# Attention stage: the keys' largest projection goes into their exponentials as a bias, four copies become reciprocals, the rest rows use another PSUM bank, and the first two steps are in an order written by hand

## The chip, the core and the metric

The kernel runs on one core of one Trainium2 chip. The metric is the device time of one execution, in microseconds (us); the median of a few executions is given. A core has five engines with a queue each, which work in their queue's order: TensorE (PE, matrix products and transposes), VectorE (DVE), ScalarE (ACT), GpSimd (POOL) and SyncE (SP, which issues the transfers here). They wait for each other by semaphores. PE writes its results to PSUM, which has eight banks of 128 x 512 float32.

## The reference

```
def phi(x):
    proj = x @ w_phi                                   # 64 -> 128 features
    proj = proj - max(abs(proj), axis=-1)              # per row
    return concat([exp(proj), exp(-proj)], -1)         # 256 features
q_p, k_p = phi(q), phi(k)                              # 4 batches, 8 heads, 576 rows
kv  = k_p^T v ;  z = sum of k_p over the rows
attn = (q_p kv) / (q_p z + 1e-6)                       # -> x, 2304 x 512
x = max(x w1, x w2, x w3) @ w_out                      # first expert layer, d_ff 768
... noisy top-2 routing of x to 8 experts, each relu(x w1[e]) w2[e], weighted sum ...
```

The weights of the layer behind the attention arrive as 64-bit numbers. The kernel makes 32-bit ones of them while the attention runs ("narrowing").

## The kernel before

The program has three stages: linear attention, the first expert layer, and the routed experts. The change touches the first alone, some 220 us of the whole.

**Steps.** The attention runs in 16 steps, one for each batch and pair of heads; `period(a)` lists what step `a` issues. Each call is entered with a time (`at(t, f, ...)`); the calls are sorted by these times, and that sorted list is the order of the queues of PE, DVE, ACT and SP. The times set an order only; nothing waits for a clock. In one period three steps overlap: step `a` is projected, step `b = a - 1` is summed into kv and z, and step `c = a - 2` gets its numerators, denominators and the division. Of the 576 rows of a head, 512 go through each step ("main rows"); the last 64 rows of two batches are put together and handled once in two steps ("rest rows", kind "r"): their projection and exponentials of the keys in the even steps, the transposition of their queries (`turn_q` of kind "r") in the odd ones.

**The path of a step.** `turn` transposes the loaded rows (PE, into a PSUM bank), `raw_in` copies them to the tile `th` (ACT), `proj` multiplies by `w_phi` (PE, keys into the banks p0 and p1, queries into s0 and s1, rest rows into s2 and t1). `peak` takes the largest absolute value of each row (DVE, tile `m`), `center` subtracts it (DVE, tiles `dk`, `dq`, `dr`). For keys, `exp_k` takes the exponentials of `dk` and of `-dk` (ACT, tile `kp`, four instructions of 128 x 512 in a step). For queries, `turn_q` transposes `dq` (PE) and `exp_q` takes the exponentials (ACT). `kv_sum` and `z_sum` sum over the rows (PE, bank k), `kv_out`, `kv_turn` and `kv_in` copy and transpose the sums (`kvT`, `kv`).

**The division.** `denom` puts the denominators into bank t0, `den_in` copies them (ACT, tile `dn`), and a chain on DVE follows: `den_turn` (a transpose, `dt`), `den_inv` (a reciprocal, `rc`), `den_copy` (four small copies within `rc`), and then twice `den_back` (`rb`) and `divide` (into `xT`), once for the numerators in bank s2 and once for those in t1. A bank that holds numerators is free when its `divide` has read it.

**Narrowing.** For each half block of the weights, SP loads `bits`, DVE makes `nm` in two instructions, ACT makes `nr`, and POOL needs four more (`narrow_end`); `narrow_out` then stores the result, or, for the first eight halves, splits it into `wh` (ACT) and `wl` (POOL). An odd step from step 3 on has two halves, an even one has one.

The banks that matter here, and the lines of the calls that the change moves:

```
A_, B_, C_, D_, E_, G_, H_ = "p0", "p1", "s0", "s1", "t0", "s2", "t1"
at(1.65, turn, a, "r", G_)            # even step: rest rows, into s2
at(2.2, turn_q, b, "r", 0, G_)        # odd step: their queries, into s2
at(8.9, numer, c, 0, G_)              # numerators, into s2
```

Of the kernel before, what the change touches and what calls it, by code (L numbers as in the profile page):

```python
# [9 lines left out]
F32 = mybir.dt.float32  # L10
# [4 lines left out]
AF = mybir.ActivationFunctionType  # L15
# [4 lines left out]
P = 128  # L20
# [3 lines left out]
class Plan:  # L24
# [5 lines left out]
    def at(self, t, f, *x):  # L30
        self.ops.append((t, len(self.ops), f, x))
# [7 lines left out]
def tile_linear_attention__then__moe__then__noisy_top2_moe(  # L39
# [20 lines left out]
    nc = tc.nc  # L60
# [17 lines left out]
    HALF = S // 2  # L78
# [11 lines left out]
    plan = Plan()  # L90
    at = plan.at
    st, pools = {}, {}
# [216 lines left out]
    ap, ain = pools["attn"], pools["ain"]  # L309
# [61 lines left out]
                         v[b, 2 * hp + h, 0:MAIN, :].rearrange("(p j) d -> p j d", j=JT))  # L371

    kps, qps = {}, {}

    def heads(s):
        u, i = divmod(s, 2)
        bb, hp = divmod(u, HP)
        return u, i, bb, hp
# [38 lines left out]
    def width(kind):  # L417
        return 2 if kind == "r" else 4
# [7 lines left out]

    def center(s, kind, g):
        n = width(kind)
        pj, m = st.pop(("pj", kind, g))[:, :n], st.pop(("m", kind, g))
        if kind == "r":  # L430
            if g == 0:
                st["d", kind] = ap.tile([P, 4, NF], F32, name="dr").rearrange(
                    "p (a h) f -> p a h f", a=2)
            d = st["d", kind][:, :, g, :]
        else:
            d = ap.tile([P, 4, NF], F32, name=f"d{kind}", bufs=2)
            st["d", kind, g] = d
        nc.vector.tensor_tensor(d, pj, m[:, :, None].to_broadcast([P, n, NF]), op=ALU.subtract)  # L438

    def exp_k(s, kind, g, sg):  # L440
        u, i, bb, hp = heads(s)
        scale = 1.0 - 2.0 * sg
        if kind == "r":
            if sg == 0:
                kps[u, "r"] = ap.tile([P, 2, 2, NF], F32, name="kp2", bufs=2)
            nc.scalar.activation(kps[u, "r"][:, :, sg, :], st["d", kind][:, 0], AF.Exp, scale=scale)
            return
        if g == 0 and sg == 0:
            kps[s] = ap.tile([P, 2, 4, 2, NF], F32, name="kp4", bufs=2)
        nc.scalar.activation(kps[s][:, g, :, sg, :], st["d", kind, g], AF.Exp, scale=scale)  # L450

    def turn_q(s, kind, g, name):
        pt = bank(name).rearrange("p (a c) -> p a c", a=4)
# [71 lines left out]
    def quarter(h, n):  # L525
        g = 2 * h + n
        return slice(g * QD, (g + 1) * QD)
# [24 lines left out]

    def den_inv(s):
        rc = ap.tile([P, 2, NB], F32, name="rc", bufs=2)
        dt_ = st.pop(("dt", s))[:, 0:HALF:32]
        nc.vector.reciprocal(rc, dt_[:, None, :].to_broadcast([P, 2, NB]))
        st["rc", s] = rc

    def den_copy(s, n):

        rc = st["rc", s]
        for h in range(2):
            nc.vector.tensor_copy(rc[quarter(h, 1 - n), n, :], rc[quarter(h, n), n, :])

    def den_back(s, n):
        rb = ap.tile([P, NB, 32], F32, name="rb", bufs=2)
# [9 lines left out]
    NS = B * HP  # L576
    STEP = 10.9
# [35 lines left out]
    def step_halves(a):  # L613

        def count(a):
            return min(a, 1) + (a % 2 if a > 2 else 0)

        n = sum(count(i) for i in range(a))
        return range(n, n + count(a) if a < NS else len(halves))

    A_, B_, C_, D_, E_, G_, H_ = "p0", "p1", "s0", "s1", "t0", "s2", "t1"

    def both(t, kind, a, at):
        for g in range(2):
            at(t + 1.4 * g, peak, a, kind, g)
            at(t + 0.7 + 1.4 * g, center, a, kind, g)

    def den_steps(t, c, at, last=False):
        at(t, den_turn, c)
        at(t + 0.5, den_inv, c)  # L630
        for n in range(2):
            at(t + 0.8, den_copy, c, n)
            at(t + 1.5 + 0.9 * n, den_back, c, n)
            at(t + 2.0 + 0.9 * n, divide, c, n)

    def loads(a, at):
        if 0 < a < NS:
            at(0.0, fill, a)
            if a == 3:
                at(0.0, routing_loads)  # L640
            if a == 2:
                at(2.0, routing_consts)
            if a + 1 < NS:
                at(0.0, load_main, a + 1)
                at(0.0, load_vals, a + 1)
            if a + 1 == 2 * HP:
                at(0.0, load_rest, 1)
        if a == 2 * HP:
            at(7.5, load_rest_v, 1)
        if a < NS:  # L650
            for i, n in enumerate(step_halves(a)):
                at(1.5 + 0.9 * i, narrow_mid, n)
                at(2.8 + 0.9 * i, narrow_end, n)
                at(9.5 + 4.0 * i, narrow_out, n)
            for n in step_halves(a + 1):
                at(8.0, narrow_load, n)

    def period(a):
        base = a * STEP
        b, c = a - 1, a - 2  # L660

        def at(t, f, *x):
            plan.at(base + t, f, *x)

        loads(a, at)
        even = a % 2 == 0
        if not even:
            at(0.0, prepare, b)
        at(0.0, turn, a, "k", A_)
        at(0.1, raw_in, a, "k")  # L670
        at(0.44, turn, a, "q", B_)
        at(0.5, raw_in, a, "q")
        if c >= 0:
            at(0.88, kv_turn, c, D_)
            at(1.0, kv_in, c)
        at(1.2, turn_q, b, "q", 0, C_)
        at(1.3, exp_q, b, "q", 0)
        if even:
            at(1.65, turn, a, "r", G_)
            at(1.7, raw_in, a, "r")  # L680
        at(1.9, turn_q, b, "q", 1, E_)
        at(2.0, exp_q, b, "q", 1)
        if not even:
            at(2.2, turn_q, b, "r", 0, G_)
            at(3.0, exp_q, b, "r", 0)
        at(2.35, proj, a, "k", (A_, B_))
        at(3.25, proj, a, "q", (C_, D_))
        both(3.4, "k", a, at)
        for g in range(2):
            for sg in range(2):  # L690
                at(4.9 + 1.4 * g, exp_k, a, "k", g, sg)
        if even:
            at(4.15, proj, a, "r", (G_, H_))
            for g in range(2):
                at(6.1 + 0.01 * g, peak, a, "r", g)
                at(6.12 + 0.01 * g, center, a, "r", g)
            for sg in range(2):
                at(7.5, exp_k, a, "r", 0, sg)
        both(7.4, "q", a, at)
        at(4.6, kv_sum, b)  # L700
        at(6.8, z_sum, b)
        at(8.0, kv_out, b)
        if c >= 0:
            at(7.9, denom, c, E_)
            at(8.95, den_in, c)
            at(8.9, numer, c, 0, G_)
            at(9.9, numer, c, 1, H_)
            den_steps(10.1, c, at)

    def opening():  # L710

        at(1.2, busy, 12)
        loads(0, at)
        at(4.0, turn, 0, "k", A_)
        at(4.1, raw_in, 0, "k", True)
        at(4.2, busy, 3)
        at(4.3, turn, 0, "q", C_)
        at(4.4, raw_in, 0, "q")
        at(4.5, turn, 0, "r", G_)
        at(4.6, raw_in, 0, "r")  # L720
        at(5.0, proj, 0, "k", (A_, B_))
        at(5.3, proj, 0, "q", (C_, D_))
        at(5.5, proj, 0, "r", (G_, H_))
        both(6.0, "k", 0, at)
        for g in range(2):
            for sg in range(2):
                at(7.0 + 1.4 * g, exp_k, 0, "k", g, sg)
        for g in range(2):
            at(9.0 + 0.01 * g, peak, 0, "r", g)
            at(9.02 + 0.01 * g, center, 0, "r", g)  # L730
        for sg in range(2):
            at(9.3, exp_k, 0, "r", 0, sg)
        both(9.3, "q", 0, at)

    at(0.0, start)
    opening()
    for s in range(1, NS):
        period(s)
    T = NS * STEP

# [709 lines left out]
    for i in range(2 * 4):  # L1450
        g, j = 1 + i // 4, i % 4
        t = END + 0.1 + i * 3.2
# [63 lines left out]
    for c in range(NCHUNK):  # L1516
        if c == 1:
            for i, job in enumerate(jobs):
                t = clock[0] + 8.0 * i
# [55 lines left out]
    for n, (e, M, row0) in enumerate(units):  # L1575
# [9 lines left out]
        if seven(n):  # L1585
            for two in ((0, 1), (2, 3)):
                for q_ in ORDER7:
                    for f in two:
                        pe(2 * 3 * HN / 2400, product, n, e, q_, f)
                        d0, d = (-0.03, 0.01) if two[0] and q_ == ORDER7[-1] else (0.02, 0.44)  # L1590
# [165 lines left out]
```

## Time and profile before

| | |
|---|---|
| median of 3 executions | 991.24 us (990.67 to 992.7) |
| the profiled execution, its own time | 993.33 us |
| its span, first to last instruction | 991.7 us |
| mean granted TensorE clock | 0.985 |
| PE busy | 956.3 us (96%) |
| DVE, ACT, POOL busy | 603.9, 453.4, 487.8 us |

The profile gives each engine's busy time; a busy share is a mean over stages with different limits. Behind the attention PE is busy nearly all the time. In the attention stage no engine is. In rows of the timeline the columns are: start in us, duration of the group in us, engine, line, operation, output<-input, shape, count; in brackets the engine's idle time just before, and what ended it. Several instructions of one form that follow each other stand in one row, with their count.

### The profile page before, as it was taken

Reading aid. Unit: us, or ns where it says so; the run is one execution under the profiler, and the core shown is the slowest. Engines: PE = TensorE matmul, PEld = TensorE weight load, DVE = VectorE, ACT = ScalarE, POOL = GpSimd, SP = SyncE. Lnnn points to the kernel's source line nnn. Section 1 sums busy time; section 2 is a strip of 40 time slices with the busy share of each in tenths; the row PEclk is TensorE's granted clock in tenths of the full one; section 3 lists DMA queues with packets and bytes.
Section 4 is the critical chain, followed back from the end, with each engine's and each line's share of the span. In section 5 each row is a group of like instructions: output and inputs, shape, how many; then the busy total and the mean of one; then the engine's idle time right before and its main releaser. Section 6 shows DMA issues by size and latency. Waiting matters only on the chain. (4 is left out here: it accounts for less than half of the span.)

```text
span 991.7 us, 19004 instructions
## 1 busy us (share of the span) xinstructions
PE 956.3 (96%) x7225; PEld 832.2 (84%) x7225; DVE 603.9 (61%) x1253; ACT 453.4 (46%) x894; POOL 487.8 (49%) x554
## 2 busy tenths in 40 slices
PE   7988889899999999999999999999999999999997
PEld 5766666678999999999998789989898989889895
DVE  4889989996435363636345425547577675756641
ACT  5766566663333333433334314427364554636350
POOL 4656666652126464464423444137374555647253
PEclk9989999999999999999999999999999999999999
DMA  7457476524245756566605355737565564838312
GB/s 202 99 167 191 128 251 187 159 69 150 64 143 174 236 171 223 182 187 189 207 4 182 93 182 165 278 97 280 169 253 193 199 248 157 293 128 302 122 32 70
DMA packets 125359, 169.19 MB, mean 171 GB/s; under 512 B 35630, under 2 KB 86958, under 8 KB 125266
## 3 DMA queue, kind: packets, MB, share of 16 engines
q1 hardware_dynamic: 114338, 138.35, 44.5%
q0 software_dynamic: 10928, 29.62, 8.7%
q8 instruction: 57, 0.93, 0.4%
q14 instruction: 36, 0.29, 0.1%
HBM read 119.38 MB, written 49.14 MB: 170 GB/s over the span
## 5 line engine op out<-in xcount | busy, mean ns | idle before, releaser
L772 PE MATMUL s<-xh,wh 128*128 128x384 f32 x432 | 147.8, 342 | 0.0
L772 PE MATMUL s<-xh,wl 128*128 128x384 f32 x432 | 145.3, 336 | 0.0
L772 PE MATMUL s<-xl,wh 128*128 128x384 f32 x432 | 145.1, 336 | 0.0
L1233 POOL DMA_INDIRECT out_dram<-o,emeta x40 | 47.4, 1185 | 128.4 <-DVE o L1231 64.4
L782 DVE TENSOR_TENSOR a<-s,a 128x384 f32<-128x384 f32 x72 | 39.9, 554 | 90.3 <-PE s L772 88.1
L1306 DVE TENSOR_TENSOR wl<-raw,wh 128x1024 fp32r<-128x1024 f32 x58 | 70.8, 1220 | 30.6 <-ACT wh L1298 26.6
L1223 PE MATMUL p<-wh,hh 128*128 128x512 f32 (+1 forms) x216 | 86.3, 400 | 0.0
L772 PEld LDWEIGHTS s<-xh,wh 128*128 128x128 f32 x432 | 81.2, 188 | 5.6 <-issue 2.2
L1223 PE MATMUL p<-wl,hh 128*128 128x512 f32 (+1 forms) x216 | 85.2, 395 | 0.0
L1223 PE MATMUL p<-wh,hl 128*128 128x512 f32 (+1 forms) x216 | 85.2, 394 | 0.0
L772 PEld LDWEIGHTS s<-xl,wh 128*128 128x128 f32 x432 | 81.2, 188 | 1.5
L772 PEld LDWEIGHTS s<-xh,wl 128*128 128x128 f32 x432 | 81.1, 188 | 0.0
L1298 ACT ACTIVATE wh<-raw 128x1024 fp32r<-128x1024 f32 x58 | 61.2, 1057 | 34.3 <-DMA raw<-in_moe_w_dram 20.0
L1276 POOL TENSOR_TENSOR raw<-raw 128x256 f32<-128x256 f32 x24 | 19.2, 800 | 110.6 <-DMA raw<-in_moe_w_dram 94.7
L210 POOL TENSOR_TENSOR nm<-nm,nr 128x512 int32<-128x512 int32 x24 | 31.4, 1309 | 73.5 <-ACT nr L202 43.7
L948 POOL DMA_INDIRECT meta<-mt,si x36 | 36.8, 1021 | 54.1 <-DVE si L944 45.0
L1081 PE MATMUL s<-gx,wh 128*128 128x304 f32 x288 | 62.1, 302 | 0.0
L130 ACT ACTIVATE hh<-a 128x384 fp32r<-128x384 f32 x36 | 18.8, 523 | 89.1 <-DVE a L782 89.1
L131 DVE TENSOR_TENSOR gx<-t,gx 128x512 fp32r<-128x512 f32 (+3 forms) x82 | 39.4, 495 | 32.8 <-ACT gx L130 32.7
L130 ACT ACTIVATE gx<-t 128x512 fp32r<-128x512 f32 (+3 forms) x82 | 34.9, 449 | 44.5 <-DVE t L1056 28.3
L1010 POOL DMA_INDIRECT gx<-x2d,emeta x28 | 28.3, 1011 | 47.9 <-PE t L1020 17.5
L450 ACT ACTIVATE kp<-dk 128x512 f32<-128x512 f32 x64 | 36.9, 629 | 30.3 <-DVE dk L438 30.3
(299 smaller groups left out, 2628.3 us busy)
## 6 DMA issues: line engine op xcount, KB each, us to landing
raw<-in_moe_w_dram SPq DMA_DIRECT2D x58, 512.0 KB
raw<-in_moe_w_dram SPq DMA_DIRECT2D x48, 256.0 KB
sums<-qh SPq DMA_DIRECT2D x24, 512.0 KB
sums<-raw SPq DMA_DIRECT2D x24, 512.0 KB
wh<-sums SPq DMA_DIRECT2D x24, 512.0 KB
wl<-sums SPq DMA_DIRECT2D x24, 512.0 KB
bits<-in_moe_w_dram SPq DMA_DIRECT2D x18, 512.0 KB
out_dram<-zrow SPq DMA_DIRECT2D x9, 512.0 KB
```

Of the source, the lines that this page charges most:

```text
L130: nc.scalar.activation(hi, src, AF.Copy)
L131: nc.vector.tensor_tensor(lo, src, hi.bitcast(F32), op=ALU.subtract)
L210: nc.gpsimd.tensor_tensor(m_, m_, r_, op=ALU.add)
L450: nc.scalar.activation(kps[s][:, g, :, sg, :], st["d", kind, g], AF.Exp, scale=scale)
L772: nc.tensor.matmul(p_, a[:, d, fs], b_, start=(n == 0), stop=(n == 3 * KD - 1))
L782: nc.vector.tensor_tensor(a, p_, st.pop("a"), op=ALU.max)
L948: ins = nc.gpsimd.indirect_dma_start(out=meta, out_offset=bass.IndirectOffsetOnAxis(ap=si[:, t, kk:kk + 1], axis=0), in_=mt[:, t, kk, :], ...
L1081: nc.tensor.matmul(bk["p"], a[:, d, fs], b_[:, d, :], start=(d == 0 and i == 0), stop=(d == 1 and i == 2))
L1223: nc.tensor.matmul(p_, a, b_[:, fw], start=(f == 0 and r == 0), stop=(f == (3 if seven(n) else F2 - 1) and r == 2))
L1233: alone(e, nc.gpsimd.indirect_dma_start(out=out, out_offset=bass.IndirectOffsetOnAxis(ap=mt[:m, i, 1:2], axis=0), in_=o[:m], in_offset=Non ...
L1298: nc.scalar.activation(WE[e, i][0], st["w2", e, i], AF.Copy)
L1306: nc.vector.tensor_tensor(wl, st.pop(("w2", e, i)), wh.bitcast(F32), op=ALU.subtract)
```

## The change

Line numbers of the kernel after are 1 to 13 higher in this part than before (`exp_k`'s new exponentials are L462, the new copy of `m` is L433).

- **Keys from step 2 on (`FOLD = 2`).** `center` no longer subtracts on DVE. ACT makes `w = -m` (128 x 4), and `exp_k` reads the projection from its PSUM bank and takes `exp(x + w)` and `exp(-x + m)`, with `w` or `m` as the bias of the ACTIVATE. A bias holds one value for each partition, so an instruction covers 128 columns instead of 512: sixteen instead of four in a step. The banks p0 and p1 stay taken until these are done, and so does the tile `m` (four buffers).
- **Reciprocals for copies.** `den_copy` took four copies of 32 x 9 from `rc`; now it takes four reciprocals of 32 x 9 from `dt`.
- **Rest rows in bank k.** `turn` and `turn_q` of kind "r" write to bank k, not to s2; in odd steps `turn_q` and `exp_q` of the rest rows stand earlier in the step.
- **Steps 0 and 1.** Step 1 is taken out of `period` and interleaved by hand with step 0.
- **Split of the first narrowed half.** `narrow_out` of step 1 moves from 9.5 to 14.9; those of the other steps go from 9.5 to 10.0.

```
 def center(s, kind, g):
     n = width(kind)
+    if kind == "k" and s >= FOLD:
+        m = st["m", kind, g]
+        w = ap.tile([P, 4], F32, name="w", bufs=2)
+        nc.scalar.activation(w, m, AF.Copy, scale=-1.0)
+        st["d", kind, g] = st.pop(("pj", kind, g)), (w, m)
+        return
...
 def exp_k(s, kind, g, sg):
...
-    nc.scalar.activation(kps[s][:, g, :, sg, :], st["d", kind, g], AF.Exp, scale=scale)
+    if s < FOLD:
+        nc.scalar.activation(kps[s][:, g, :, sg, :], st["d", kind, g], AF.Exp, scale=scale)
+        return
+    pj, m = st["d", kind, g]
+    for a in range(4):
+        nc.scalar.activation(kps[s][:, g, a, sg, :], pj[:, a, :], AF.Exp, scale=scale,
+                             bias=m[sg][:, a:a + 1])
...
 def den_copy(s, n):
-        nc.vector.tensor_copy(rc[quarter(h, 1 - n), n, :], rc[quarter(h, n), n, :])
+        nc.vector.reciprocal(rc[quarter(h, 1 - n), n, :], st["dt", s][quarter(h, n), 0:HALF:32])
...
 loads(a, at):
-            at(9.5 + 4.0 * i, narrow_out, n)
+            at((14.9 if a == 1 else 10.0) + 4.0 * i, narrow_out, n)
...
 period(a):
-            at(1.65, turn, a, "r", G_)
+            at(1.65, turn, a, "r", "k")
-            at(2.2, turn_q, b, "r", 0, G_)
-            at(3.0, exp_q, b, "r", 0)
+            at(1.65, turn_q, b, "r", 0, "k")
+            at(1.7, exp_q, b, "r", 0)
...
 opening(): steps 0 and 1
+        at(7.1, turn, 1, "k", E_)
+        at(8.2, turn, 1, "q", "k")
+        at(10.2, proj, 1, "k", (A_, B_))
+        both(12.0, "k", 1, at)
+        both(13.4, "q", 1, at)
+        at(11.2, proj, 1, "q", (C_, D_))
+        at(12.6, kv_sum, 0)
...
-    for s in range(1, NS):
+    for s in range(2, NS):
```

ACT's queue in an odd step. Before, from the narrowing's copy of the first half (L202) to the denominators' copy (L543), it stands so:

```order
L202 ACTIVATE nr<-bits 128x512
L465 ACTIVATE qp_1864<-t_1903 128x2x256 x2
L202 ACTIVATE nr<-bits 128x512
L470 ACTIVATE qp_1864<-s_1911 128x2x64
L470 ACTIVATE qp_1865<-s_1911 128x2x64
L470 ACTIVATE qp_1864<-s_1911 128x2x64
L470 ACTIVATE qp_1865<-s_1911 128x2x64
```

Behind these stand the four exponentials of the keys (L450), `kvT` and `dn`. In the kernel after, the same place of step 9 begins with the last of the rest rows' four exponentials (L483, from bank k) and ends with `dn` (L556):

```order
L483 ACTIVATE qp_1952<-k 128x2x64
L478 ACTIVATE qp_1951<-t_1997 128x2x256 x2
L202 ACTIVATE nr<-bits 128x512
L433 ACTIVATE w<-m 128x4
L462 ACTIVATE kp_2065<-p_2005,w 128x128 x4
L462 ACTIVATE kp_2065<-p_2005,m 128x128 x4
L433 ACTIVATE w<-m 128x4
L462 ACTIVATE kp_2065<-p_2006,w 128x128 x4
L462 ACTIVATE kp_2065<-p_2006,m 128x128 x4
L512 ACTIVATE kvT<-k 128x384
L556 ACTIVATE dn<-t_2106 128x288
```

The rest rows' exponentials have moved ahead of `exp_q` of the second half of the queries, and four key exponentials have become sixteen with two copies of `m` between them; `kvT` and `dn` stand behind them all as before.

PE's queue at the start of an even step: before,

```order
L506 MATMUL s_1260<-ident,kvT 128x128 x3
L456 MATMUL s_1267<-ident,dq 128x128 x4
L392 MATMUL s_1281<-ident,kl 128x128
L392 MATMUL s_1281<-ident,ql 128x128
L456 MATMUL t_1286<-ident,dq 128x128 x4
```

and after:

```order
L519 MATMUL s_1311<-ident,kvT 128x128 x3
L469 MATMUL s_1318<-ident,dq 128x128 x4
L393 MATMUL k<-ident,kl 128x128
L393 MATMUL k<-ident,ql 128x128
L469 MATMUL t_1337<-ident,dq 128x128 x4
```

The order is the same; the two transposes of the rest rows write bank k instead of s2. The next instruction of the step that writes s2 is then `proj` of the rest rows, behind the projections of the keys and queries.

DVE's queue from the maxima of an even step to the second division, after:

```order
L424 TENSOR_REDUCE m<-p_914 128x4
L424 TENSOR_REDUCE m<-p_915 128x4
L424 TENSOR_REDUCE m<-s_944 128x2
L424 TENSOR_REDUCE m<-t_945 128x2
L445 TENSOR_TENSOR dr<-s_944,m 128x2x128
L445 TENSOR_TENSOR dr<-t_945,m 128x2x128
L424 TENSOR_REDUCE m<-s_930 128x4
L445 TENSOR_TENSOR dq<-s_930,m 128x512
L424 TENSOR_REDUCE m<-s_931 128x4
L445 TENSOR_TENSOR dq<-s_931,m 128x512
L563 STREAM_TRANSPOSE dt<-dn 128x288
L569 RECIPROCAL rc<-dt 128x18
```

Before, a subtraction `dk<-p,m` of 128 x 512 stood behind each of the first two rows, and right behind the last row shown `COPY rc<-rc 32x9 x4` stood where `RECIPROCAL rc<-dt 32x9 x4` stands now. The maximum of the first queries (`m<-s_930`) is the fifth `m` of the step; its buffer is the one that the first group of key exponentials reads as bias. SP's queue is the same before and after.

## Rows read from the trace of the kernel before

**Rows 1.** Windows: start:end, length, busy us (count) by engine, clock, DMA share, GB/s.

```profile
38.28:212.31 174.03, 154.53 (x2406) 114.99 (x2402) 158.21 (x299) 111.07 (x241) 107.91 (x85) 0.94 0.56 164
212.31:991.70 779.39, 770.90 (x4444) 693.92 (x4440) 423.72 (x914) 320.08 (x607) 360.91 (x428) 1.00 0.53 172
96.00:106.83 10.83, 10.83 (x185) 7.97 (x181) 10.36 (x19) 7.68 (x18) 7.22 (x7) 1.00 0.47 91
106.83:123.19 16.36, 13.17 (x194) 9.98 (x190) 14.57 (x31) 9.10 (x19) 8.82 (x7) 0.90 0.50 144
161.44:174.35 12.91, 11.87 (x193) 8.70 (x190) 12.44 (x23) 8.09 (x17) 8.87 (x8) 1.00 0.83 258
```

**Rows 2.** Timeline of PE, in the even steps 8 and 12.

```profile
112.07 0.33 PE L392 MATMUL s<-ident,kl 128*128 128x128 f32 x1 [2.82 <-DVE xT L573]
...
112.89 2.08 PE L413 MATMUL p<-wphi,th 64*128 64x128 f32 x16
...
164.31 0.33 PE L392 MATMUL s<-ident,kl 128*128 128x128 f32 x1 [1.01 <-DVE xT L573]
...
165.12 1.16 PE L413 MATMUL p<-wphi,th 64*128 64x128 f32 x16
```

**Rows 3.** Timeline of DVE, steps 6 to 9.

```profile
94.64 0.48 DVE L550 STREAM_TRANSPOSE dt<-dn 128x288 f32<-128x288 f32 x1
...
95.45 1.60 DVE L563 COPY rc<-rc 32x9 f32<-32x9 f32 x4
...
100.05 1.35 DVE L190 TENSOR_SCALAR nm<-bits 128x512 int32<-128x512 int32 x1
101.44 1.41 DVE L199 SCALAR_TENSOR_TENSOR nm<-bits,nm 128x512 int32<-128x512 int32 x1
102.78 0.68 DVE L423 TENSOR_REDUCE m<-p 128x4 f32<-128x512 f32 x1
103.49 0.69 DVE L438 TENSOR_TENSOR dk<-p,m 128x512 f32<-128x512 f32 x1
...
108.06 0.47 DVE L550 STREAM_TRANSPOSE dt<-dn 128x288 f32<-128x288 f32 x1
108.57 0.27 DVE L556 RECIPROCAL rc<-dt 128x18 f32<-128x18 f32 x1
108.87 2.08 DVE L563 COPY rc<-rc 32x9 f32<-32x9 f32 x4
...
113.57 0.46 DVE L573 TENSOR_TENSOR xT<-t,rb 128x288 f32<-128x288 f32 x1
...
122.64 0.71 DVE L563 COPY rc<-rc 32x9 f32<-32x9 f32 x4
```

**Rows 4.** Timeline of POOL, steps 7 and 8.

```profile
107.90 1.49 POOL L212 TENSOR_SCALAR nr<-nr 128x512 f32<-128x512 f32 x1
109.47 1.27 POOL L213 TENSOR_TENSOR nm<-nm,nr 128x512 f32<-128x512 f32 x1
```

**Rows 5.** Timeline of ACT, step 15.

```profile
206.73 0.85 ACT L470 ACTIVATE qp<-s 128x128 f32<-128x128 f32 x4
207.36 2.37 ACT L450 ACTIVATE kp<-dk 128x512 f32<-128x512 f32 x4
209.63 0.47 ACT L499 ACTIVATE kvT<-k 128x384 f32<-128x384 f32 x1
```

**Rows 6.** Groups of ACT to 232 us: busy us, mean ns, idle before.

```profile
L470 ACT ACTIVATE qp<-s 128x128 f32<-128x128 f32 x32 | 6.7, 343 | 0.0
...
L588 ACT ACTIVATE warm<-warm 128x1 f32<-128x1 f32 x1 | 0.2, 203 | 0.0
```

**Rows 7.** Timeline of the opening, steps 0 to 2.

```profile
19.68 0.43 DVE L190 TENSOR_SCALAR nm<-bits 128x512 int32<-128x512 int32 x1 [4.02 <-DMA bits<-in_moe_w_dram]
...
20.14 0.69 DVE L199 SCALAR_TENSOR_TENSOR nm<-bits,nm 128x512 int32<-128x512 int32 x1
...
26.42 0.52 PE L506 MATMUL s<-ident,kvT 128*128 128x128 f32 x3 [2.06 <-DVE dq L438]
```

More of the change, by code (lines that the diff above doesn't have):

```diff
@@ L373, in tile_linear_attention__then__moe__then__noisy_top2_moe @@
     kps, qps = {}, {}
+    FOLD = 2
     def heads(s):
@@ L554, in den_inv @@
         rc = ap.tile([P, 2, NB], F32, name="rc", bufs=2)
-        dt_ = st.pop(("dt", s))[:, 0:HALF:32]
+        dt_ = st["dt", s][:, 0:HALF:32]
         nc.vector.reciprocal(rc, dt_[:, None, :].to_broadcast([P, 2, NB]))
@@ L710, in opening, with exps, later @@
     def opening():
+        def exps(t, a):
+            for g in range(2):
+                for sg in range(2):
+                    at(t + 1.3 * g + 0.6 * sg, exp_k, a, "k", g, sg)
+        loads(0, at)
+        def later(t, f, *x):
+            plan.at(STEP + t, f, *x)
+        loads(1, later)
+        at(0.0, prepare, 0)
         at(1.2, busy, 12)
-        loads(0, at)
         at(4.0, turn, 0, "k", A_)
@@ L716, in opening @@
         at(4.2, busy, 3)
[L717 to L720, printed above, removed]
         at(5.0, proj, 0, "k", (A_, B_))
-        at(5.3, proj, 0, "q", (C_, D_))
-        at(5.5, proj, 0, "r", (G_, H_))
+        at(5.1, turn, 0, "q", C_)
+        at(5.2, raw_in, 0, "q")
+        at(5.3, busy, 2)
+        at(6.0, proj, 0, "q", (C_, D_))
+        at(7.0, turn, 0, "r", "k")
+        at(7.1, turn, 1, "k", E_)
+        at(8.0, raw_in, 0, "r")
+        at(8.1, proj, 0, "r", (G_, H_))
+        at(8.2, turn, 1, "q", "k")
+        at(9.4, raw_in, 1, "k")
+        at(10.0, raw_in, 1, "q")
+        at(10.2, proj, 1, "k", (A_, B_))
         both(6.0, "k", 0, at)
+        exps(7.5, 0)
+        both(8.0, "q", 0, at)
         for g in range(2):
[L726 to L730, printed above, removed]
-        for sg in range(2):
-            at(9.3, exp_k, 0, "r", 0, sg)
-        both(9.3, "q", 0, at)
+            at(10.8 + 0.01 * g, peak, 0, "r", g)
+            at(10.82 + 0.01 * g, center, 0, "r", g)
+        both(12.0, "k", 1, at)
+        both(13.4, "q", 1, at)
+        at(11.0, turn_q, 0, "q", 0, E_)
+        at(11.1, exp_q, 0, "q", 0)
+        at(11.2, proj, 1, "q", (C_, D_))
+        at(11.3, turn_q, 0, "q", 1, G_)
+        for sg in range(2):
+            at(12.2, exp_k, 0, "r", 0, sg)
+        at(12.3, exp_q, 0, "q", 1)
+        at(12.4, turn_q, 0, "r", 0, H_)
+        at(12.5, exp_q, 0, "r", 0)
+        at(12.6, kv_sum, 0)
+        at(12.7, z_sum, 0)
+        exps(13.0, 1)
+        at(16.0, kv_out, 0)
     at(0.0, start)
     opening()
-    for s in range(1, NS):
+    for s in range(2, NS):
         period(s)
```

## The prediction, made before the kernel was run

> **What bounds the kernel now.** I read the windows first. Behind the attention, from 212.31 us on, PE is busy for 770.90 of 779.39 us [rows 1], so what the attention saves or loses comes out at the end one to one. Steps 3 to 15 are one window of 174.03 us, at a mean clock of 0.94. The odd steps in it are all alike: one takes 10.83 us, PE is busy for all of it and the granted clock is 1.00. PE bounds those. The even steps are not: step 8 takes 16.36 us with PE busy for 13.17 and a clock of 0.90, step 12 takes 12.91 us with PE busy for 11.87 at a clock of 1.00 [rows 1].
>
> The timeline of PE names the difference [rows 2]. In step 8 PE stands for 2.82 us before the transpose of the rest keys, until `divide` has read bank s2, and the projection behind that takes 2.08 us; in step 12 the same wait is 1.01 us and the same projection takes 1.16 us. So PE is let down by DVE, and then it also loses its upper clock level (2.4 GHz) for a while. DVE's timeline shows why the division is late [rows 3]: it goes from one instruction to the next, and the four copies in `rc`, 0.71 us at 122.64, take 2.08 us at 108.87, where POOL is busy up to 110.74 [rows 4]. The reciprocal before them ran in the middle of POOL's L212 and took 0.27 us.
>
> **The cover of the odd steps.** PE alone needs 10.83 us for an odd step and 12.91 - 1.01 = 11.9 for an even one, 22.7 us for a pair [rows 1, 2]. Below that the pair can't go by this change. Now 12 steps, 4 to 15, take 174.03 - 10.83 = 163.2 us, 27.2 a pair.
>
> **The ring through DVE and ACT.** A pair can't be shorter than the ring either in which DVE waits for ACT's `dn` and ACT for DVE's maxima. I go round it once, with the names of the code.
>
> 1. From `dt` of an even step to the first maximum of the next odd step: 102.78 - 94.64 = 8.14 us now, with 1.60 for the copies and 1.35 + 1.41 for a second narrowing that meets POOL [rows 3]. Four reciprocals instead of the copies: below, 0.71, as the copies alone; above 4 x 0.27 = 1.1 [rows 3]. I take 0.8, nearer the copies, since both are of 32 x 9. That leaves 7.3 us.
> 2. From that maximum to `dt` of the odd step. DVE now needs 5.3 us (102.78 to 108.06) [rows 3]. Without the two subtractions of 0.69 it needs 3.9, and then it waits for ACT: the maximum 0.7, a hand-over 0.2, two copies of `m`, sixteen exponentials, `kvT` 0.5 [rows 5] and `dn`, which I put at 0.4 after it. A copy of 128 x 4 is nearest to the 0.203 us of a 128 x 1 [rows 6]; the exponential behind it reads its result, so I count 0.25 each. With p for one exponential that is 2.3 + 16p.
> 3. From `dt` of the odd step to the end of the second division: 113.57 + 0.46 - 108.06 = 5.97 us now, less 2.08 for the copies, plus 0.8: 4.7 us [rows 3]. The even step's first maximum follows.
> 4. From there to `dt` of the even step: as in 2, and the rest rows' two exponentials of 256 columns, 0.6 (half of four of 512, 209.63 - 207.36 = 2.27 [rows 5]): 2.9 + 16p.
>
> Together 17.2 + 32p; 1.6 less where the second narrowing finds POOL idle (1.35 + 1.41 against the 0.43 + 0.69 of the opening [rows 3, 7]).
>
> **The price of an exponential, p.** This decides. Four now cost 2.27 us for 512 columns each, from SBUF. The nearest row to the new ones are the four of 128 x 128 from PSUM: they follow each other by (207.36 - 206.73) / 4 = 0.16 us [rows 5], and one of them lasts 0.343 us [rows 6]. None of these takes its bias from a tile. So p lies between 0.16 (the bias costs nothing) and 0.34 (nothing overlaps any more). I take the middle, 0.25: an operand more has to be fetched, and I have no row for it. At 0.25 the sixteen cost 4.0 us, with the copies of `m` 4.5, against 2.27 now: ACT pays 2.2 us in a step to take 2 x 0.69 from DVE [rows 3, 5].
>
> The Trainium skill has a price here (ScalarE: Activation LUTs, "What ACT_TABLE_LOAD costs"): an ACTIVATE whose bias is a pointer to one value per partition takes about 93 ns longer than one with an immediate. On 0.16 that gives an estimate of 0.25, and the sum would be the one below; by the row alone it would be that of the first rival. No row here shows it.
>
> **The sum.** At p = 0.25 the ring takes 25.2 us, or 23.6 with POOL idle. The second narrowing meets POOL in five of the seven odd steps now (one of them is in [rows 3]), so I take 24.6. That is above PE's 22.7, so the ring is the new bound, and PE waits in the even step: about 1 us before the queries' transpose into p1 (taken until the last exponential of the step before) and about 1 us before `proj` of the rest rows, which now meets the wait for `divide`, but stands behind both other projections. Waits of 1.01 us left the clock at 1.00 [rows 1, 2], so I count no slow projections.
>
> - Six pairs (steps 4 to 15): 6 x 24.6 = 147.6. In steps 4 and 6 POOL also makes `wl` and is still busy when DVE narrows, which costs the 1.6 each: 3.2. Together 150.8 against 163.2: -12.4 us.
> - Step 3: odd, PE is its bound, 0.
> - The opening: DVE now waits 4.02 us for `bits` before step 1's maxima, and PE waits 2.06 in step 2 for the last subtraction [rows 7]; L228 stands in ACT's queue ahead of step 2's copies. The new order takes the first maximum before the wait and moves L228 behind the copies; `bits` itself comes no earlier, since SP's queue is as before. I take -1.2, between 0 and the 2.06.
> - New waits: in odd steps `kv_sum` waits in bank k for the rest rows' exponentials. These last 0.85 us together [rows 5], and ACT's narrowing, which may wait for `bits`, stands ahead of them. Between nothing and 0.85 a pair; I take nothing, since PE has slack in a pair of 24.6. In even steps DVE's maximum of the queries waits for the `m` that the first eight exponentials read, with the second maximum and `dt` behind it; the ring has `dt` later anyway.
> - The four edits of 9.5 to 10.0 change no queue: 0. The transfers have to come in 8% less time; the DMA share over the steps is 0.56 [rows 1], so I count nothing.
>
> -13.6 us from the profiled execution's 993.33 is 979.7. That execution is 2.1 us above the median, so I predict **978 us**.
>
> **Rivals.**
> - *The bias costs nothing* (p = 0.16). The ring is 22.3, PE's 22.7 bounds: 6 x 22.7 + 1 for POOL's extra work in steps 4 and 6 = 137.2, -26.0, with the opening -27.2: 964 us. For it: the row of the same shape. Against it: that row has no such operand.
> - *The exponentials don't overlap* (p = 0.34). Ring 28.1; six of them and the 3.2 are 171.8 against 163.2: +8.6, with the opening +7.4: 999 us, slower. It turns at p = 0.30, where the ring is (163.2 + 1.2 - 3.2) / 6 = 26.9. The change then takes PE's wait away and gives ACT more than that.
> - *The wait only moves*: `proj` of the rest rows stands over 2 us for `divide`, and the clock falls as in step 8, whose PE busy time is 1.3 us above step 12's [rows 1]. Or the reciprocals wait for POOL as the copies did, 1.3 us a pair. Either is +8 on the forecast: 986 us.
> - *No effect*: ACT's price just eats what PE gets back, 991 us. It needs p at 0.3.
>
> **How the numbers follow.** The forecast has 0.50 (p from 0.2 to 0.3, 970 to 984 us), the first rival 0.23 (961 to 969), the moved wait 0.12 (984 to 989), no effect 0.07, the slower one 0.08. A measurement of this kernel can tell about 0.2%, that is 989.3 and 993.2 us: faster 0.85, same 0.07, slower 0.08. The range of 963 to 988 us leaves out the slower cases and the ends of the fast one.
>
> **What would show it.** In the profile after: the exponentials L462 at 0.25 us from start to start; no wait of PE before the transposes into bank k; waits of about 1 us before `qm` and before `proj` of the rest rows in even steps; the four reciprocals below 1.2 us with POOL busy; odd steps still near 10.8 us and even ones near 13.8, at a clock of 1.00. The prediction is wrong if L462 comes well below 0.2 or above 0.3, if even steps still show projections of 2 us, or if odd steps become longer because ACT's copies `th` are late.

## The result, and the profile after

The kernel after takes 976.75 us (median of 4 executions, 976.07 to 977.91), beside 991.34 us (990.67 to 992.7) for the kernel before on the same chip: a ratio of 0.985, 95% interval 0.984 to 0.987. It is faster by 14.6 us, 1.5%; 978 were forecast.

The windows of the kernel after, in the columns of [rows 1]: steps 3 to 15 (the last to 10.75 us from its start, the length of an odd step), the rest of the attention, all behind it, and then steps 4, 7, 8 and 9.

```profile
36.13:195.70 159.57, 147.67 (x2405) 108.94 (x2401) 131.36 (x272) 136.18 (x419) 109.02 (x84) 1.00 0.61 179
195.70:205.17 9.47, 7.70 (x144) 5.04 (x140) 6.93 (x16) 8.01 (x19) 4.53 (x4) 1.00 0.36 112
205.17:974.40 769.23, 762.48 (x4305) 689.19 (x4301) 416.51 (x901) 314.51 (x596) 359.08 (x424) 1.00 0.53 173
46.87:61.34 14.47, 12.30 (x194) 8.94 (x190) 10.39 (x24) 13.79 (x43) 11.58 (x10) 1.00 0.84 260
86.31:97.06 10.75, 10.75 (x186) 8.00 (x182) 10.17 (x20) 8.64 (x27) 7.98 (x6) 1.00 0.68 165
97.06:110.97 13.91, 11.97 (x194) 8.78 (x190) 9.90 (x23) 12.17 (x39) 8.90 (x8) 1.00 0.59 164
110.97:121.70 10.73, 10.73 (x186) 7.99 (x182) 10.13 (x20) 8.54 (x27) 6.70 (x5) 1.00 0.89 282
```

The stage of 174.03 us [rows 1] takes 159.57, and its clock is 1.00 where it was 0.94. Odd steps are as they were; the even step 8 takes 13.91 us, not 16.36. DVE's busy time has fallen from 158.21 to 131.36 us, ACT's has risen from 111.07 to 136.18. Of the profiled execution's 17.3 us (991.7 to 974.4), 2.15 lie ahead of step 3 and 14.5 in steps 3 to 15; the tail up to the expert layer (PE's first product of `wh` at 205.17, before at 219.95) gives 1.8 back; the last 2.5 lie behind the attention, which the change leaves as it was. In the fourteen profiled executions of the table below this stretch takes 769.2 to 771.8 us, most in the kernel before, whose profiled execution stood 2.1 us above its median.

PE's timeline of step 8, beside [rows 2]:

```profile
98.54 0.66 PE L393 MATMUL p<-ident,qm 128*128 128x128 f32 x4 [0.82 <-ACT kp L462]
...
99.79 0.27 PE L393 MATMUL k<-ident,kl 128*128 128x128 f32 x1
...
100.54 1.16 PE L414 MATMUL p<-wphi,th 64*128 64x128 f32 x16
...
104.03 0.37 PE L414 MATMUL t<-wphi,th 64*128 64x128 f32 x1 [1.11 <-DVE xT L586]
...
104.67 1.93 PE L499 MATMUL k<-kp,vt 128*32 128x256 f32 x32
```

The wait of 2.82 us before the rest keys is gone and their projection follows at the upper clock level. In its place stand the two waits that the prediction named, 0.82 us before `qm` and 1.11 us before `proj` of the rest rows.

DVE's timeline, steps 7 to 9, beside [rows 3]:

```profile
99.19 0.48 DVE L563 STREAM_TRANSPOSE dt<-dn 128x288 f32<-128x288 f32 x1 [2.21 <-ACT dn L556]
...
100.01 0.88 DVE L576 RECIPROCAL rc<-dt 32x9 f32<-32x9 f32 x4
...
107.05 0.69 DVE L424 TENSOR_REDUCE m<-s 128x4 f32<-128x512 f32 x1 [0.55 <-ACT kp L462]
...
110.64 0.48 DVE L563 STREAM_TRANSPOSE dt<-dn 128x288 f32<-128x288 f32 x1 [0.85 <-ACT dn L556]
...
117.69 1.27 DVE L424 TENSOR_REDUCE m<-p 128x4 f32<-128x512 f32 x2
...
123.82 0.48 DVE L563 STREAM_TRANSPOSE dt<-dn 128x288 f32<-128x288 f32 x1 [2.21 <-ACT dn L556]
...
128.51 1.28 DVE L424 TENSOR_REDUCE m<-p 128x4 f32<-128x512 f32 x2
...
135.26 0.48 DVE L563 STREAM_TRANSPOSE dt<-dn 128x288 f32<-128x288 f32 x1 [0.85 <-ACT dn L556]
```

DVE now waits for ACT's `dn`, 2.21 us in these odd steps and 0.85 in the even ones, and in even steps 0.55 us for the exponentials that read `m`; before, `dt` came right behind the maxima at 94.64 and 108.06. The four arcs of the predicted ring can be read off: 110.64 to 117.69 is 7.05 us (forecast 7.3), to 123.82 it is 6.13 (6.3), to 128.51 4.69 (4.7), to 135.26 6.75 (6.9): 24.62 us a pair.

ACT's timeline in step 9, which has p:

```profile
118.63 1.14 ACT L462 ACTIVATE kp<-p,w 128x128 f32<-128x128 f32 x4
119.64 1.16 ACT L462 ACTIVATE kp<-p,m 128x128 f32<-128x128 f32 x4
120.64 0.26 ACT L433 ACTIVATE w<-m 128x4 f32<-128x4 f32 x1
120.93 1.14 ACT L462 ACTIVATE kp<-p,w 128x128 f32<-128x128 f32 x4
```

Four exponentials take 119.64 - 118.63 = 1.01 us: p = 0.25.

### The profile page after: what moved, and what is told of

Read it like the earlier page. It is cut to its first block, busy times and chain, and to the rows that moved or that the text cites. A ratio compares the mean times of both kernels' runs of the same rounds, so it can differ in the third digit from the quotient of the medians.

```text
span 974.4 us, 19190 instructions
## 1 busy us (share of the span) xinstructions
PE 947.1 (97%) x7227; PEld 825.0 (85%) x7227; DVE 575.4 (59%) x1225; ACT 482.3 (49%) x1090; POOL 490.7 (50%) x554
## 5 line engine op out<-in xcount | busy, mean ns | idle before, releaser
L1339 ACT ACTIVATE wh<-raw 128x1024 fp32r<-128x1024 f32 x58 | 61.1, 1056 | 30.7 <-DMA raw<-in_moe_w_dram 15.7
L1264 PEld LDWEIGHTS p<-wh,hl 128*128 128x128 f32 (+1 forms) x216 | 40.8, 189 | 9.3
```

The costliest lines, as they stand in the source:

```text
L1264: nc.tensor.matmul(p_, a, b_[:, fw], start=(f == 0 and r == 0), stop=(f == (3 if seven(n) else F2 - 1) and r == 2))
L1339: nc.scalar.activation(WE[e, i][0], st["w2", e, i], AF.Copy)
```

## The experiments

Two theories stood against each other. **Theory A:** the gain comes from the rest rows' bank and the reciprocals; the bias trades a little of DVE's work for more of ACT's and closes a ring through `dn`, so that by itself it is worth nothing or less. **Theory B:** the gain is DVE's relief by the bias. All ratios are to the kernel before on the same chip, whose medians were 991.3, 991.5 and 989.9 us beside e1 to e4, beside e5_rest_alone to e9, and beside the other four.

| run | median us | ratio, 95% interval | step 3 starts | steps 4 to 14 | step 15 and tail |
|---|---|---|---|---|---|
| before | 991.3 | 1 | 38.28 | 152.47 | 18.37 |
| after | 976.75 | 0.985 (0.984 to 0.987) | 36.13 | 138.08 | 20.22 |
| e1_no_fold | 971.96 | 0.980 (0.979 to 0.982) | 36.08 | 134.13 | 19.93 |
| e2_copies | 988.53 | 0.998 (0.997 to 0.999) | 36.63 | 151.75 | 18.62 |
| e3_rest_s2 | 981.29 | 0.991 (0.989 to 0.992) | 36.57 | 140.73 | 20.21 |
| e4_old_opening | 977.86 | 0.986 (0.985 to 0.988) | 37.23 | 138.12 | 20.22 |
| e5_rest_alone | 982.86 | 0.991 (0.990 to 0.993) | 37.09 | 142.65 | 19.90 |
| e6_recip_alone | 975.52 | 0.984 (0.982 to 0.985) | 37.82 | 134.44 | 18.94 |
| e6_plain | 965.95 | 0.976 (0.974 to 0.978) | 37.56 | 126.27 | 18.44 |
| e7_half_fold | 969.34 | 0.978 (0.976 to 0.979) | 37.59 | 131.15 | 18.39 |
| e9_fold_dn | 966.89 | 0.975 (0.974 to 0.977) | 36.14 | 128.89 | 18.38 |
| e10_half_dn | 966.39 | 0.976 (0.975 to 0.978) | 35.83 | 127.25 | 18.38 |
| e11_fold_dn_m8 | 965.36 | 0.975 (0.974 to 0.977) | 35.88 | 129.13 | 18.38 |
| e12_last_unfolded | 977.86 | 0.987 (0.985 to 0.989) | 39.84 | 137.71 | 19.87 |

The last three columns are from each profiled execution, from PE's first transposes of `km` in steps 3, 4 and 15 and its first product of the expert layer.

### One part of the change undone

**e1_no_fold.**

```
-    FOLD = 2
+    FOLD = 16
```

> The kernel after with FOLD = 16: every step subtracts on DVE and takes four exponentials of 128x512 again; all other edits stay. Theory A (the gain comes from the rest rows' bank k and the four reciprocals; the bias only trades DVE's 2 x 0.69 us a step for 2.2 us of ACT, and the ring through DVE and ACT stays near 24 us a pair): steps 3 to 15 take 154 to 161 us at a clock of 1.00, 973 to 978 us in all. Theory B (the gain comes from the relief of DVE by the bias): pairs go back to 26 us or more, DVE shows no wait for dn, and the kernel takes 985 to 990 us.

Measured: 971.96 us, 4.8 us faster than the whole change, with intervals that don't touch. Steps 4 to 14 take 134.13 us, not 138.08. The windows of steps 8 and 9, and DVE's timeline of step 9:

```profile
96.45:109.49 13.04, 11.84 (x193) 8.71 (x190) 12.47 (x28) 8.82 (x19) 8.91 (x8) 1.00 0.62 179
109.49:120.28 10.79, 10.79 (x186) 8.00 (x182) 10.25 (x21) 7.65 (x18) 6.71 (x5) 1.00 0.88 276
```

```profile
120.95 0.69 DVE L445 TENSOR_TENSOR dq<-s,m 128x512 f32<-128x512 f32 x1
121.56 0.47 DVE L563 STREAM_TRANSPOSE dt<-dn 128x288 f32<-128x288 f32 x1
```

DVE does the two subtractions again and has no wait in its list from 36 to 190 us; `dt` follows `dq` at once. A pair takes 13.04 + 10.79 = 23.83 us, beside 24.62 with the bias. With it DVE saves 4 x 0.69 = 2.76 us in a pair and waits 2.21 + 0.85 + 0.55 = 3.61; the difference is about the 0.8 by which a pair is longer. So the bias as placed here is a loss. B falls, and A's mechanism stands, though it expected 973 us or more.

**e2_copies.**

```
-  nc.vector.reciprocal(rc[quarter(h, 1 - n), n, :], st["dt", s][quarter(h, n), 0:HALF:32])
+  nc.vector.tensor_copy(rc[quarter(h, 1 - n), n, :], rc[quarter(h, n), n, :])
```

> The kernel after with den_copy's four copies from rc in place of the four reciprocals. Theory A (they stand on the ring, between dt and the next maxima): in odd steps the four take 2.1 us again where POOL is busy, each pair is 1.2 us longer, six pairs 7 us: 983 to 985 us. Rival (DVE has 2.2 us of wait for dn in an odd step, which takes them up): no pair changes, 976 to 978 us.

Measured: 988.53 us, 11.8 more than the kernel after; four fifths of the gain are gone. In step 8, DVE's copies, where POOL is busy:

```profile
107.62 1.71 DVE L576 COPY rc<-rc 32x9 f32<-32x9 f32 x4
```

and PE's timeline:

```profile
110.55 0.46 PE L414 MATMUL s<-wphi,th 64*128 64x128 f32 x2 [0.23 <-DVE xT L586]
112.47 0.37 PE L414 MATMUL t<-wphi,th 64*128 64x128 f32 x1 [1.46 <-DVE xT L586]
...
113.10 3.48 PE L499 MATMUL k<-kp,vt 128*32 128x256 f32 x32
```

The window of the step:

```profile
104.67:121.09 16.42, 13.91 (x194) 9.57 (x190) 11.64 (x27) 12.34 (x39) 8.89 (x8) 0.90 0.49 141
```

The copies take 0.83 us more than the reciprocals (1.71 beside 0.88). PE's wait before `proj` of the rest rows then lasts 0.23 + 1.46 = 1.69 us, not 1.11, and behind it the sums over the keys take 3.48 us, not 1.93: PE has fallen to its lower clock level (the step's granted clock is 0.90). So 0.83 us of copies cost 2.5 us in the step (16.42 beside 13.91). Theory A's place was right, its size (983 to 985 us) too small: it had priced the copies and not the clock. In step 8 the kernel after stood half a microsecond of waiting from the prediction's third rival.

**e3_rest_s2.**

```
-  at(1.65, turn, a, "r", "k")
+  at(1.65, turn, a, "r", G_)
-  at(1.65, turn_q, b, "r", 0, "k")
-  at(1.7, exp_q, b, "r", 0)
+  at(2.2, turn_q, b, "r", 0, G_)
+  at(3.0, exp_q, b, "r", 0)
```

> The kernel after with the rest rows' transposes in bank s2 and at their old places; the bias and the reciprocals stay. Theory A: the bank is a large part of the gain: PE waits again for divide before the transpose of the rest keys in even steps, the granted clock there falls, even steps take 15 us or more, and the kernel 983 to 990 us. Theory B (the gain is DVE's relief, which makes divide early anyhow): PE's wait there is under 1 us, the clock stays at 1.00, and the kernel takes 976 to 979 us.

Measured: 981.29 us, 4.5 more than after, a little less than A expected. PE in step 8 waits again before the rest keys:

```profile
103.28 0.33 PE L393 MATMUL s<-ident,kl 128*128 128x128 f32 x1 [1.92 <-DVE xT L586]
```

The wait is 1.92 us here, 12.1 in six even steps, so B's "under 1 us" is wrong. A is right in part: the clock falls in steps 6 and 12, which take 16.00 and 16.06 us, and stays at 1.00 in the other four. Windows of steps 6 and 10:

```profile
72.78:88.78 16.00, 13.19 (x193) 9.69 (x189) 11.11 (x27) 13.98 (x42) 12.03 (x10) 0.89 0.67 202
123.55:138.01 14.46, 11.60 (x193) 8.40 (x190) 10.49 (x24) 12.35 (x39) 8.82 (x7) 1.00 0.79 252
```

PE waits 0.75 and 2.06 us in step 6, 0.80 and 2.06 in step 10: the same waits cost the clock once and not the other time, and what decided isn't shown. Steps 4 to 14 are 2.65 us longer than in the kernel after; PE's listed waits from 36 to 190 us sum to 15.3 us beside 11.9.

**e4_old_opening:** the opening of the kernel before in the kernel after, and `for s in range(1, NS)`.

> The kernel after with the opening of the kernel before, and step 1 by the pattern of all steps. The opening was taken at 1.2 us; step 3 begins 2.15 us earlier in the kernel after. Theory A: all of this is the new order's: step 3 begins at 38.3 us again, and the kernel takes 978 to 979 us. Rival (the earlier start comes from the bias and the reciprocals in step 2): step 3 begins near 36.5 us, 976.5 to 977.5 us.

Measured: 977.86 us, 1.1 more, with intervals that overlap. Step 3 starts at 37.23 us, between the two theories, but single executions don't settle this. With the new opening step 2 took 12.1 to 14.0 us in seven profiled executions, all at a granted clock of 1.00, and 15.7 to 16.8 in three (e6_plain, e7 and e12), at 0.80 to 0.89. In the kernel before it took 15.72 us at 0.89, in e4 12.23 at 1.00. So the earlier start of step 3 has the clock of step 2 in it, and how much of it is the new order's is not shown.

### One part of the change alone

**e5_rest_alone, e6_recip_alone.** The kernel before with the rest rows in bank k (the edit of e3 the other way), and the kernel before with the reciprocals (the edit of e2 the other way).

> The kernel before with one edit alone: the rest rows in bank k (both lines, with their new places). The copies stay, and so do the subtractions. Theory A as it stands now (two things pay, and each needs the other: the reciprocals shorten DVE's chain, the bank lets PE's wait come behind two projections): the wait of 2.8 us goes from the transpose of the rest keys to their projection and is shorter there by the 2 us of the two projections ahead, but with copies of 2.08 us it stays over 1.5 us, the clock falls in the even steps, and the kernel takes 983 to 990 us. Rival (the bank alone is the gain): no wait over 1.2 us, clock 1.00, 972 to 978 us.

> The kernel before with one edit alone: four reciprocals for the four copies. Theory A: divide comes 1.2 us earlier in an even step where POOL was busy, PE's wait before the transpose of the rest keys falls from 2.8 to 1.6 us, which still lets the clock fall in some even steps: 976 to 984 us. Rival (without the bank nothing is gained, since the wait still stands in PE's way at the clock's cost): 987 us or more.

Measured: 982.86 us with the bank alone, 8.6 less than the kernel before beside it, and 975.52 us with the reciprocals alone, 15.9 less: alone the reciprocals bring as much as the whole change. Two rows of PE in step 8, of the bank alone and of the reciprocals alone:

```profile
106.94 0.37 PE L413 MATMUL t<-wphi,th 64*128 64x128 f32 x1 [1.46 <-DVE xT L573]
...
107.58 3.49 PE L486 MATMUL k<-kp,vt 128*32 128x256 f32 x32
```

```profile
100.36 0.33 PE L392 MATMUL s<-ident,kl 128*128 128x128 f32 x1 [1.33 <-DVE xT L573]
```

With the bank alone the wait moves behind the projections and costs the clock, as in e2, in three of six even steps (4, 8 and 10, at 0.89); in step 14 the clock stays at 1.00 after the same 0.23 and 1.46 us. With the reciprocals alone the wait stays where it was and is halved, and the sums take 1.93 us in all steps but step 4, where the clock is 0.89. Theory A as it stood here, that each of the two needs the other, is wrong: they relieve the same wait, and the reciprocals do nearly all of it. From e6_recip_alone to e1_no_fold, which adds the bank and the opening, steps 4 to 14 go only from 134.44 to 134.13 us. The bank and the reciprocals without the new opening were not run.

### The price of the operand

**e6_plain.**

```
-  nc.scalar.activation(kps[s][:, g, a, sg, :], pj[:, a, :], AF.Exp, scale=scale,
-                       bias=m[sg][:, a:a + 1])
+  nc.scalar.activation(kps[s][:, g, a, sg, :], pj[:, a, :], AF.Exp, scale=scale)
```

> The kernel after without the bias operand in the sixteen exponentials, so that the keys' maximum is left out of them (w is still made); what it tells is the price of the operand. Theory A: they follow each other by 0.16 us as the four of the same shape do, the ring is 2.9 us a pair shorter, PE's work sets the pairs at 22 to 22.7 us, and the kernel takes 962 to 967 us. Rival (the price is that of the pieces, not of the operand): 0.25 us as before, 976 to 978 us.

Measured: 965.95 us. ACT's timeline of step 9:

```profile
114.53 1.44 ACT L462 ACTIVATE kp<-p 128x128 f32<-128x128 f32 x8
115.78 0.27 ACT L433 ACTIVATE w<-m 128x4 f32<-128x4 f32 x1
```

Eight follow each other in 115.78 - 114.53 = 1.25 us, 0.16 each, as the four of [rows 5]. So the operand costs 0.25 - 0.16 = 0.09 us, sixteen times a step, and that is what turned the first rival (964 us) into the forecast.

The Trainium skill (ScalarE: Activation LUTs, "What ACT_TABLE_LOAD costs") gives about 93 ns for a bias read through a pointer; the two runs agree with it, at 0.09 us.

### What closes the ring, and what is left

**e7_half_fold.** The bias for g = 0 only; g = 1 goes through DVE as before.

```
-  if kind == "k" and s >= FOLD:
+  if kind == "k" and s >= FOLD and g == 0:
...
-  if s < FOLD:
+  if s < FOLD or g == 1:
```

> The kernel after, but only the first half of the keys (g = 0, bank p0) gets its maximum as a bias; the second half is subtracted on DVE and takes two exponentials of 128x512. Theory A (without the bias DVE is the whole ring, 23.8 us a pair with no wait; with the bias in both halves ACT's dn is late by 2.2 and 0.85 us; in between both are shorter): DVE saves 0.69 us a step, dn comes about 0.35 us later than without the bias, pairs of 23.0 to 23.4 us, 967 to 970 us. Rival (each half of the bias costs half of the loss): halfway between 972 and 976.8, 974 us.

Measured: 969.34 us, better than with no bias and with all of it. DVE's waits for `dn` fall from 19.2 us (36 to 190 us) to 3.9. The halfway time of the rival is refuted: each half of the bias takes the same off DVE, but it is the second that makes `dn` late. The 969.34 us lie in A's range.

**e9_fold_dn.** All of the bias, but `kvT` and `dn` ahead of the second half's exponentials, and the queries turned in bank t0.

```
-  at(4.9 + 1.4 * g, exp_k, a, "k", g, sg)
+  at(4.9 + 4.2 * g, exp_k, a, "k", g, sg)
-  at(0.44, turn, a, "q", B_)
+  at(0.44, turn, a, "q", E_)
```

> The kernel after with the bias in both halves, and two moves: kvT and dn ahead of the second half's eight exponentials in ACT's queue, and the queries transposed into bank t0, so that they don't wait for these in p1. Theory A (dn behind sixteen exponentials is what closes the ring): DVE's waits for dn vanish, the ring falls by 1 to 2 us a pair to 22.7 to 23.5, 964 to 971 us. Rival (ACT has simply too much to do: 136 us busy in 159.6, its copies th then come late, and PE waits for them): pairs stay at 24.6 us, 975 to 978 us.

Measured: 966.89 us, 9.9 less than the kernel after with the same instructions on every engine. ACT's timeline in an odd step, then the wait lists (36 to 190 us; total, times, longest): DVE's in the kernel after, DVE's for `m` and PE's here:

```profile
140.84 0.25 ACT L433 ACTIVATE w<-m 128x4 f32<-128x4 f32 x1
140.93 0.54 ACT L512 ACTIVATE kvT<-k 128x384 f32<-128x384 f32 x1
141.30 0.47 ACT L556 ACTIVATE dn<-t 128x288 f32<-128x288 f32 x1
141.59 1.22 ACT L462 ACTIVATE kp<-p,w 128x128 f32<-128x128 f32 x4
```

```profile
DVE dt L563 <- ACT dn L556: 19.2, 13, 2.2
DVE m L424 <- ACT kp L462: 3.3, 6, 0.6
```

```profile
DVE m L424 <- ACT kp L462: 4.8, 6, 1.3
```

```profile
PE t L469 <- ACT th L403: 4.7, 4, 1.5
PE t L414 <- DVE xT L586: 0.7, 1, 0.7
```

DVE waits for `dn` nowhere any more, as the ring has it: the same sixteen exponentials cost 10 us less when `dn` doesn't stand behind eight of them. The two moves were not run apart. What speaks for the order and not the bank is that DVE's list of the kernel after names no wait for PE, so that PE's wait for p1 was not on the ring. The rival is right in part: PE now waits for ACT's `th` in four steps.

**e10_half_dn, e11_fold_dn_m8.** The edits of e7 and e9 together; and e9 with `name="m", bufs=8` for 4.

> The kernel after with the bias in the first half of the keys alone, kvT and dn ahead of the second half's two exponentials, and the queries transposed into bank t0. Theory A (the ring closes through dn, and ACT is the next bound when both halves have the bias): DVE waits for nothing, ACT has 1.1 us a step less to do than with the bias in both halves, PE's work alone sets the pairs, 21.9 us (10.73 + 11.17, the even steps without a wait in the run before): 960 to 965 us. Rival (nothing is left between 22.7 and the floor that these moves could give): the same as with the bias in both halves, 966 to 968 us.

> The run with the bias in both halves, dn early and the queries in t0, and eight buffers of m in place of four. Theory A: DVE's wait of 0.56 us (up to 1.3) for the m that the first half's exponentials read is on the ring of the even steps, now that dn is early: 4.8 us of waits go, of which 2 to 4 come out: 963 to 965 us. Rival (ACT's work sets the pace): 966 to 968 us.

Measured: 966.39 and 965.36 us. With e9 and e6_plain they can't be told apart (intervals from 0.974 to 0.978). In e11 DVE's waits for `m` are gone, and 4.6 us for `dn` have come in their place; steps 4 to 14 take 129.13 us beside e9's 128.89, which speaks for the rival, though 965.36 lies between the two ranges. In e10 the 960 to 965 us of A are missed: its floor is reached in some even steps but not in all, as two windows show, step 8 and step 6:

```profile
93.18:106.24 13.06, 11.69 (x193) 8.70 (x190) 12.47 (x28) 10.07 (x26) 8.92 (x8) 1.00 0.63 177
71.28:82.45 11.17, 11.17 (x193) 8.43 (x190) 10.62 (x26) 10.02 (x27) 10.70 (x9) 1.00 0.61 174
```

In step 8 PE waits 1.37 us for `divide`. In the step before it DVE makes its second narrowing while POOL is busy, the difference that the prediction had put at 1.6 us a pair:

```profile
86.52 1.30 DVE L190 TENSOR_SCALAR nm<-bits 128x512 int32<-128x512 int32 x1
87.86 1.42 DVE L199 SCALAR_TENSOR_TENSOR nm<-bits,nm 128x512 int32<-128x512 int32 x1
```

Both narrowings of step 7 take DVE 4.43 us, those of step 5 3.19; and `dt` comes 0.59 us after the start of step 8, but 0.62 before that of step 6. Step 8's own narrowing, ahead of the second `divide`, takes 1.82 us, step 6's 1.11. That this makes the steps of 13 us was not tried by itself.

**e12_last_unfolded.**

```
-  if kind == "k" and s >= FOLD:
+  if kind == "k" and FOLD <= s < NS - 1:
...
-  if s < FOLD:
+  if not FOLD <= s < NS - 1:
```

> The kernel after with the bias in steps 2 to 14 alone; step 15 subtracts on DVE as before. Theory A (kvT of step 14 stands behind the sixteen exponentials of step 15, and PE has nothing else then): PE's wait of 1.77 us behind step 15 goes to under 0.5 us, and the kernel takes 975 to 976 us. Rival (DVE is late there as well): the wait stays, 976.5 to 977.5 us.

Measured: 977.86 us, no gain; the wait stays, as the rival had it. PE's wait behind step 15, in the kernel after and in e12:

```profile
197.52 0.55 PE L519 MATMUL s<-ident,kvT 128*128 128x128 f32 x3 [1.77 <-ACT kvT L512]
```

```profile
200.53 0.52 PE L519 MATMUL s<-ident,kvT 128*128 128x128 f32 x3 [1.45 <-DVE dq L445]
```

With the bias PE lacks `kvT`, which stands behind sixteen exponentials; without it PE lacks bank s1, from which DVE subtracts last. In e7, e9, e10 and e11, with `kvT` behind fewer exponentials and fewer subtractions on DVE, step 15 and the tail take 18.4 us, as before the change.

## Why the prediction was right

It forecast 978 us, and 976.75 came.

- **PE let down by DVE, the clock behind it:** right. e2 and e5 bring back wait and lower level with the copies; in e2's step 8, 0.6 us of waiting more costs 2.5 us.
- **The ring, 17.2 + 32p:** right, arc by arc, within 0.25 us each; steps 7 to 14 come in pairs of 24.6 to 24.7 us, the value taken. That the value fits so well is luck: it was 25.2 us less 0.6 for odd steps in which POOL is idle, but the second narrowing is slow in all seven odd steps (0.84 to 1.00 and 1.41 to 1.43 us), and the arcs themselves were 0.6 us shorter together. e9 bears the ring out by opening it.
- **p = 0.25:** right. The row without the operand alone would have given 0.16 and the first rival, as e6_plain shows. The value was the middle of a range, and not read from a row.
- **The copies of `m`, 0.25 us, and the reciprocals, 0.8:** 0.20 to 0.26, and 0.88 with POOL busy or idle.
- **ACT pays 2.2 us in a step to take 2 x 0.69 from DVE:** right, and worth more than a remark: from the first copy to `kvT` step 9 needs 122.94 - 118.39 = 4.55 us. The prediction didn't draw the conclusion that the change without the bias would be faster; e1 is, by 4.8 us.
- **Steps 4 and 6, 3.2 us for POOL's `wl`:** mis-sized. They take 14.47 and 14.24 us beside 13.9: 0.9 together. DVE's narrowing there takes 0.77 + 0.69 and 0.78 + 0.69 us, against 0.42 + 0.69 in the other even steps: 0.35 more each, not 1.6.
- **PE's floor of 22.7 us a pair:** too high. 12.91 - 1.01 was taken for an even step without a wait; e9, e10 and e11 show such steps at 11.17, a pair at 21.9. The forecast didn't rest on it, the first rival did.
- **The opening, -1.2:** the start of step 3 came 2.15 us earlier, but the clock of step 2, 0.89 before and 1.00 after, is in that; the order's share is not shown (e4).
- **The tail, not in the sum:** PE loses 1.8 us behind step 15, for `kvT`. Against it stand 0.95 us more from the opening and 2.3 less in steps 4 and 6; that the forecast came within 1.3 us is in part luck.
- **Moved wait, the third rival:** didn't come, but was near. The waits that came in step 8, 0.82 and 1.11 us, kept the clock at 1.00; e2's, with 0.58 more, did not, and in e3 and e5 the same waits cost it in one step and not in another.
- **The slower rival's 999 us:** its ring of 28.1 lacks the 0.6 that the forecast had taken off its own; with it the same sum gives 995.

## What to carry to other kernels

Follow the ring before you take work off an engine that seems full: taking 1.4 us a step from DVE put 2.2 us more of ACT's work in front of an instruction for which DVE then waited. With half of these exponentials behind `dn`, and the queries in another bank, the same work was 10 us faster. Split a change of several edits by its parts: here the four reciprocals alone gave as much as the whole. Half a microsecond more of waiting on TensorE cost 2.5 us where the clock fell behind it (e2), so price a small delay by what stands just behind the wait too.

## What was not expected of the hardware

A reciprocal of 32 x 9 took 0.22 us whatever POOL did (0.88 for four in the kernel after, at 100.01 us with POOL busy and at 111.45 with POOL idle), while copies of the same shape took 0.71 to 2.08 us for four ([rows 3], and 1.71 in e2). Rows of POOL and DVE in the kernel after:

```profile
99.87 1.27 POOL L213 TENSOR_TENSOR nm<-nm,nr 128x512 f32<-128x512 f32 x1
...
114.75 1.28 POOL L210 TENSOR_TENSOR nm<-nm,nr 128x512 int32<-128x512 int32 x1 [6.25 <-ACT nr L202]
```

```profile
111.45 0.88 DVE L576 RECIPROCAL rc<-dt 32x9 f32<-32x9 f32 x4
```

The longer instruction was the cheaper one wherever POOL was busy. The Trainium skill (SBUF — State Buffer, "Who interferes with whom") says that copies can enter a mode in which they contend with GpSimd, and that a VectorE instruction with at most one SBUF input and outside such modes does not. The rows agree with it for the copies, and for the reciprocals if these run outside such modes, which no run here shows.
